# Routing a mixture of experts behind an attention: low parts of weights in halves, and the next round's maxima inside the tail of this one

## The chip, the cores and the metric

The kernel runs on one core of one Trainium2 chip. The metric is the device time of one execution in microseconds (us), as the median of several runs. Five engines work side by side, each through its own list of instructions, and wait for one another by semaphores: TensorE (PE in the profile; PEld is its loading of stationary operands), VectorE (DVE), ScalarE (ACT), GpSimd (POOL) and SyncE (SP, which here only starts transfers).

## The reference, cut to what matters

A local attention (4 batches, 8 heads, 768 positions, head size 64; window 16, and 24 block summaries) gives x of 3072 rows by 512. The rest is a mixture of 8 experts with a hard capacity:

```
def _moe_ref(x, w_gate, w1, w2):
    N, D = x.shape                     # 3072, 512
    E = w_gate.shape[1]                # 8
    cap = N // E                       # 384
    logits = x @ w_gate
    order = np.argsort(-logits.flatten())
    for idx in order:                  # greedy, from the largest logit down
        tok, e = (int(idx) // E, int(idx) % E)
        if assigned[tok] >= 0 or counts[e] >= cap:
            continue
        assigned[tok] = e
        counts[e] += 1
    for e in range(E):
        mask = assigned == e
        h = np.maximum(x[mask] @ w1[e], 0.0)     # 384 x 1024
        out[mask] = h @ w2[e]                    # 384 x 512
    return out
```

All experts get exactly 384 rows, and which rows they get depends on all the others.

## The kernel before

**Stages.** The attention takes about the first 145 us and writes x to memory and the logits to the tile `L` (128 x 24 tokens x 8 experts). After that come eight experts, one after the other. Expert r may only start when routing round r has said which expert fills up next (`widx`) and which rows it gets (`idx`). Round 0 runs alone, ahead of expert 0. Rounds 1 to 7 run under experts 0 to 5, cut into steps that are put between the matmuls of the experts.

**A round.** `aim` takes for each token the best logit among the experts still open (`best`), turns it into an integer key (`m`, `key`, `dup`), compares it with the first table of pivots (`g`), and finds which expert it belongs to (`cand`, `tgt`, one-hot `oh`). `search` then finds a threshold in six digits. A digit is 24 matmuls of the tables `g` with `oh` on TensorE (L449), `full` on VectorE (L451), one matmul with `steps` (L454), and on VectorE `piv`, two new tables `g` and `below` (L458 to L462). Between the third and the fourth digit stand `d`, `d`, `dup`, two `g` and `wh`. Behind the sixth come `wl`, `d`, `w`, `sel`, `widx`, two `ge` and two `inc` (L494 to L508), then two matmuls called px here (L522, L523), `place`, `to`, four `span`, the work of `spent` (which strikes out used-up experts in `WA`: `pos`, `keep`, `keep`, `WA`), twelve matmuls with `span` (L554, called at here), and `hit`, `m`, `hit`, `idx`. `close` (`wsum`, `pen`, `L`) takes the expert that is full out of `L`, and the next round's `aim` can begin.

**An expert.** Every fp32 operand is split into a high part (fp32r, made by ScalarE) and a low part (the difference, made by VectorE), and a product is three matmuls: high by high and the two mixed ones. The parts are `xh`, `xl` (gathered and transposed rows), `ah`, `al` (w1, four chunks), `hh`, `hl` (the hidden layer, 8 slices f), and `bh`, `bl` (w2, four chunks). The first half of an expert is 96 matmuls of 128 x 384, numbered h0 to h95 below, twelve for each slice f. The second half is 72 matmuls of 128 x 512, y0 to y71, nine for each f. The sums of the first half lie in three banks (`psum.tile(..., name="h", bufs=3)`, L744). So the matmuls of slice f + 3 can start only when `hh` and `hl` of slice f have been read out of the bank: h36 needs `hl` of f = 0, h48 that of f = 1, h60 that of f = 2, h72 that of f = 3. Rows for the next expert are transposed in four flips of three matmuls each (`flip_x`, L614) near the end of the second half, through one single bank `xt` (L615): a flip needs the `xl` of the flip before it, and that needs its `xh`.

**What sets the order.** Each engine works through its list strictly as the program writes it. The writing is done by a small planner in the kernel: `spend` adds the planned time of each matmul to `state["now"]`, `service` then writes out the delayed low parts in `later` whose due time has come (`hl` 1.1, `al` and `bl` 1.6, `xl` 1.1 after their high part was written), and calls `advance`, which writes the next step of the round once `state["ready"]` has passed. All of a step's VectorE instructions go into the list together. The numbers behind `yield` say after how long the next step's matmuls may be written. `prepare` starts the transfers of the next expert, its splits and its flips.

Of the kernel before, what the change touches and what calls it, by code (L numbers as in the profile page):

```python
# [33 lines left out]
NT = N // 128  # L34
VD = D + 1
TUNE = dict(
    hop=0.22, dv=1.0, e5=2, e50=0, warm2=3.6192, adv=14, y0=2.6, y1=0.3, y2=0.45,
    y2m=0.021, y3=1.7, y4=1.5, y5=1.6, y7=1.1, lo=1.1, sp=1.6, qx=23.421, aw=9.0, as_=2.6,
# [18 lines left out]
def attention_moe(ctx, tc, qT, kT, v65, wg, w1r, w2r, cst, out, dbg=None, dbi=None):  # L57
# [52 lines left out]

    def aim(T, t0, t1, last=False):
        n = t1 - t0
        best, cand, tgt = T["best"][:, t0:t1], T["cand"][:, t0:t1], T["tgt"][:, t0:t1]
        nc.vector.tensor_reduce(best, L[:, t0:t1], axis=AX.X, op=OP.max)
        ranks, experts = [], [
            lambda: nc.vector.tensor_tensor(cand, L[:, t0:t1], best[:, :, None].to_broadcast([128, n, E]), op=OP.is_equal),
            lambda: nc.vector.tensor_tensor(cand, cand, WA[:, t0:t1], op=OP.mult),
            lambda: nc.vector.tensor_reduce(tgt, cand, axis=AX.X, op=OP.max),
            lambda: nc.vector.tensor_scalar(tgt, tgt, 0.5, None, op0=OP.max)]
        if not last:  # L120
            m, key = T["m"][:, t0:t1], T["key"][:, t0:t1]
            bits = T["best"].bitcast(I32)[:, t0:t1]
            ranks = [
                lambda: nc.vector.tensor_scalar(m, bits, 31, 0x7FFFFFFF, op0=OP.arith_shift_right, op1=OP.bitwise_and),
                lambda: nc.vector.scalar_tensor_tensor(key, bits, 0x8000, m, op0=OP.bitwise_xor, op1=OP.bitwise_xor),
                lambda: nc.vector.tensor_copy(T["dup"][:, t0:t1], T["halves"][:, t0:t1, 1:2].to_broadcast([128, n, 2])),
                lambda: compare(T["g"], T["dup"], T["piv"], T["digits"][0], t0, t1)]
            experts.append(lambda: nc.vector.tensor_tensor(T["oh"][:, t0:t1], cand, tgt[:, :, None].to_broadcast([128, n, E]), op=OP.is_equal))
        for pair in zip_longest(ranks, experts):
            for op in pair:  # L130
                if op:
                    op()

# [331 lines left out]

    ROUND = {}

    def route(r):
        T = first
        if r:  # L470
            T = targets(r)
            aim(T, 0, NT, r == E - 1)
            yield 0.0, TUNE["y0"]
        R = psum.tile([128, 512], F32, name="r")
# [40 lines left out]

        late = TUNE["e5"] if r else TUNE["e50"]
        if r < E - 1 and not late:
            close()
        ROUND[r] = [widx, None]
        yield 0.03, TUNE["y4"]  # L520
        px = R[:, 32:34]
# [9 lines left out]
        def spent():  # L531
            if r == E - 1:
                return
            if late == 1:
                close()
            keep = rt.tile([128, NT], F32, name="keep", bufs=2)
            pos = rt.tile([128, NT], F32, name="pos", bufs=2)
            nc.vector.tensor_tensor(pos, place[:, 0, :NT], place[:, 1, :NT], op=OP.add)
            nc.vector.tensor_scalar(keep, pos, 0.5, None, op0=OP.is_lt)
            nc.vector.scalar_tensor_tensor(keep, pos, CAP + 0.5, keep, op0=OP.is_gt, op1=OP.add)  # L540
            nc.vector.tensor_tensor(WA, WA, keep[:, :, None].to_broadcast([128, NT, E]), op=OP.mult)
        m = ff.tile([128, 3, NT], F32, name="m3", bufs=2)
        hit = ff.tile([128, 3, NT + 1], F32, name="hit", bufs=2)
        idx = rt.tile([128, 3], I32, name="idx", bufs=E)
        for k in kinds:
            nc.vector.tensor_scalar(span[:, k, 0], count, px[:, k:k + 1], None, op0=OP.is_ge)
            nc.vector.tensor_scalar(span[:, k, 1], count, to[:, k:k + 1], -1.0, op0=OP.is_ge, op1=OP.mult)
        if r:
            spent()
        yield 0.05, TUNE["y5"]  # L550
        todo = [(k, i) for k in kinds for i in range(2)]
# [6 lines left out]
        with nc.allow_low_precision("integers below 2^24"):  # L558
            nc.vector.tensor_reduce(idx, hit, axis=AX.X, op=OP.add)
        if r == 0:  # L560
            spent()
        ROUND[r][1] = idx
        if r < E - 1 and late == 2:
            close()
# [19 lines left out]
    def split_w(r, nm, j, n=1, wait=TUNE["wlo"]):  # L584
        raw = RAW.pop((r, nm, j))
        hi = ff.tile([128, 1024], F32R, name=nm + "h", bufs=4)
        lo = ff.tile([128, 1024], F32R, name=nm + "l", bufs=4)
        WT[r, nm, j] = hi, lo
        for k in range(n):
            c = slice(k * 1024 // n, (k + 1) * 1024 // n)  # L590
            nc.scalar.activation(hi[:, c], raw[:, c], AF.Copy)  # L591

            def low(c=c):
                nc.vector.tensor_tensor(lo[:, c], raw[:, c], hi[:, c].bitcast(F32), op=OP.subtract)  # L594
# [18 lines left out]

    def flip_x(r, d):  # L614
        pt = psum.tile([128, 3, 128], F32, name="xt")  # L615
        for c in range(3):
            flip4(pt[:, c], XG[r, c][:, d * 128:(d + 1) * 128])
        split_x(r, d, pt)

    def split_x(r, d, pt):  # L620
        if d == 0:
            XT[r] = [ff.tile([128, 4, CAP], F32R, name=n) for n in ("xh", "xl")]
        xh, xl = XT[r]
        p = pt.rearrange("p c k -> p (c k)")
        nc.scalar.activation(xh[:, d], p, AF.Copy)  # L625

        def low():
            nc.vector.tensor_tensor(xl[:, d], p, xh[:, d].bitcast(F32), op=OP.subtract)
            vector(0.55)
        later.append((state["now"] + TUNE["xlo"], low))  # L630

# [3 lines left out]

    def flush():
        for it in later[:]:
            later.remove(it)
            it[1]()

    def service():
        while True:
            for it in [x for x in later if x[0] <= state["now"]]:
                later.remove(it)
                it[1]()
            if state["done"] < E - 1 and state["ready"] <= state["now"]:
# [91 lines left out]
    def expert(r):  # L738
# [3 lines left out]
        hl = ff.tile([128, 8, CAP], F32R, name="hl")  # L742
        for f in range(8):
            ph = psum.tile([128, CAP], F32, name="h", bufs=3)  # L744
            wh, wl = (w.rearrange("p (j d k) -> p j d k", j=2, d=4)[:, f % 2] for w in WT[r, "a", f // 2])
# [9 lines left out]
            def low(f=f, ph=ph):  # L755
                nc.vector.scalar_tensor_tensor(hl[:, f], ph, 0.0, hh[:, f].bitcast(F32), op0=OP.max, op1=OP.subtract)  # L756
                vector(0.55)
            later.append((state["now"] + TUNE["lo"], low))
            if f % 2 == 0:
                later.append((state["now"] + TUNE["sp"], lambda f=f: split_w(r, "b", f // 2)))  # L760
        py = [psum.tile([128, DM], F32, name="y", bufs=3) for c in range(3)]
# [84 lines left out]
```

## Time and profile before

| | us |
|---|---|
| median of 3 runs | 507.22 |
| the runs | 507.22, 510.45, 506.15 |
| the profiled execution | 508.25 |
| its span in the trace | 506.5 |
| TensorE busy in it | 463.3 |
| VectorE busy | 330.1 |
| ScalarE busy | 214.4 |
| granted TensorE clock, mean over the span | 0.95 |

The span runs from the first to the last instruction of the trace; the 1.75 us that the execution took beyond it lie around it. In a row of the timeline stand start, length (both in us), engine, line, operation, the tile written and the tiles read, and in brackets the engine's idle time ahead of it with what ended that wait. Rows of windows give for each engine the busy time in the stretch and the number of instructions, then the granted clock of TensorE.

### The profile page before, as it was taken

What the parts mean: (1) busy time and instruction counts of PE and PEld (TensorE: products, weight loads), DVE (VectorE), ACT (ScalarE), POOL (GpSimd) and SP (SyncE); (2) the same over time, 40 slices, a digit from 0 to 9 for tenths busy, and PEclk for the clock granted to TensorE, in tenths of its full rate; (3) what the DMA queues carried; (4) which work ended last, traced back from release to release, by engine and by line L of the source; (5) the groups of instructions that cost most, each with busy time, mean ns of one, the idle gap of its engine ahead of it and who ended that gap; (6) DMA issues with size and microseconds to landing.
All of it is one profiled execution on the core that took longest, in us unless ns stands there. A gap on an engine that the chain in (4) does not pass through costs nothing.

```text
span 506.5 us, 13149 instructions
## 1 busy us (share of the span) xinstructions
PE 463.3 (91%) x5160; PEld 388.6 (77%) x5160; DVE 330.1 (65%) x1293; ACT 214.4 (42%) x450; POOL 131.7 (26%) x199
## 2 busy tenths in 40 slices
PE   3799999999973899989989999899999999999993
PEld 2568687877853798779768878877987998988982
DVE  3278789977866786757865966777778462362510
ACT  1277667876810441243323513342351453453410
POOL 9547743614220300220202302300400500402011
PEclk8799999999985699979998999999999999999997
DMA  8999969211110821920641733723535445531001
GB/s 264 315 303 297 320 221 312 91 51 44 65 65 6 295 96 38 323 98 1 231 167 63 249 146 104 272 84 154 180 109 184 127 162 169 180 111 42 22 21 41
DMA packets 24157, 76.28 MB, mean 151 GB/s; under 512 B 3488, under 2 KB 3744, under 8 KB 23712
## 3 DMA queue, kind: packets, MB, share of 16 engines
q1 hardware_dynamic: 18336, 56.58, 33.9%
q0 software_dynamic: 5760, 18.88, 10.7%
q8 instruction: 40, 0.66, 0.6%
q14 instruction: 21, 0.17, 0.1%
HBM read 62.86 MB, written 12.58 MB: 149 GB/s over the span
## 4 chain that ended last, share of the span: by engine, by line
PE 73%; DVE 13%; issue 7%; POOL 4%; DMA 1%; ACT 0%; POOLq 0%; SPq 0%; ACTq 0%; DVEq 0%
PE h L749 21%; PE y L766 19%; PE o L348 5%; PE t L135 5%; PE s L312 5%; PE r L449 5%; PE x L135 2%; PE x L269 2%; PE l L354 2%; PE xt L135 2%; POOL vw L204 2%; DVE al L594 2%; DVE g L107 2%; POOL out L732 1%; PE x L279 1%
## 5 line engine op out<-in xcount | busy, mean ns | idle before, releaser
L766 PE MATMUL y<-bl,hh 128*128 128x512 f32 x192 | 78.6, 409 | 0.0
L766 PE MATMUL y<-bh,hl 128*128 128x512 f32 x192 | 77.4, 403 | 0.0
L766 PE MATMUL y<-bh,hh 128*128 128x512 f32 x192 | 76.6, 399 | 0.0
L732 POOL DMA_INDIRECT out<-y,idx x24 | 23.9, 996 | 197.6 <-ACT y L730 193.4
L753 ACT ACTIVATE hh<-h 128x384 fp32r<-128x384 f32 x64 | 31.5, 492 | 89.7 <-PE h L749 88.9
L749 PE MATMUL h<-xh,ah 128*128 128x384 f32 x256 | 60.5, 352 | 1.3 <-DVE hl L756 1.3
L327 ACT ACTIVATE pe<-sm,mx 128x118 f32<-128x118 f32 x192 | 57.7, 384 | 8.3 <-DVE mx L320 8.1
L749 PE MATMUL h<-xh,al 128*128 128x384 f32 x256 | 58.1, 346 | 0.0
L749 PE MATMUL h<-xl,ah 128*128 128x384 f32 x256 | 56.8, 340 | 0.0
L756 DVE SCALAR_TENSOR_TENSOR hl<-h,hh 128x384 fp32r<-128x384 f32 x64 | 35.3, 552 | 30.9 <-ACT hh L753 30.9
L320 DVE CUSTOM_DVE_ANT_0 sm<-s,cs 128x118 f32<-128x118 f32 x192 | 41.6, 275 | 17.1 <-PE s L312 16.3
L605 POOL DMA_INDIRECT xg<-xd,idx x24 | 25.5, 1064 | 96.5 <-issue 67.5
L625 ACT ACTIVATE xh<-xt 128x384 fp32r<-128x384 f32 x28 | 13.8, 491 | 82.4 <-PE xt L135 82.4
L749 PEld LDWEIGHTS h<-xh,ah 128*128 128x128 f32 x256 | 46.2, 194 | 2.8 <-DVE hl L756 1.7
L591 ACT ACTIVATE ah<-raw 128x1024 fp32r<-128x1024 f32 (+1 forms) x36 | 32.7, 957 | 32.0 <-DMA raw<-w1r 29.4
L749 PEld LDWEIGHTS h<-xh,al 128*128 128x128 f32 x256 | 46.1, 193 | 0.0
L749 PEld LDWEIGHTS h<-xl,ah 128*128 128x128 f32 x256 | 45.3, 189 | 0.0
L449 PEld LDWEIGHTS <-g 128*128 128x128 bf16 x1008 | 28.8, 97 | 18.0 <-DVE g L107 7.6
L766 PEld LDWEIGHTS y<-bh,hh 128*128 128x128 f32 x192 | 36.4, 190 | 6.8
L766 PEld LDWEIGHTS y<-bh,hl 128*128 128x128 f32 x192 | 36.4, 190 | 5.7
L766 PEld LDWEIGHTS y<-bl,hh 128*128 128x128 f32 x192 | 36.2, 188 | 5.8
L594 DVE TENSOR_TENSOR al<-raw,ah 128x1024 fp32r<-128x1024 f32 (+1 forms) x36 | 38.7, 1099 | 2.5 <-ACT ah L591 2.5
(129 smaller groups left out, 789.5 us busy)
## 6 DMA issues: line engine op xcount, KB each, us to landing
raw<-w1r SPq DMA_DIRECT2D x32, 512.0 KB, 4.5
raw<-w2r SPq DMA_DIRECT2D x32, 512.0 KB, 4.3
vw<-v SPq DMA_DIRECT2D x48, 195.0 KB, 7.7
kd<-kT SPq DMA_DIRECT2D x16, 399.0 KB, 5.8
xd<-x POOLq DMA_DIRECT2D x24, 256.0 KB, 3.6
qt<-qT SPq DMA_DIRECT2D x3, 1536.0 KB, 9.8
qt<-qT SPq DMA_DIRECT2D x3, 512.0 KB, 5.5
xg<-xd,idx POOLq DMA_INDIRECT x24, 3.7
```

Source lines behind the costliest of these rows:

```text
L135: nc.tensor.transpose(o, i, idn)
L320: nc.vector.tensor_tensor_reduce(sm[:, p], PS[u][:, p], m, -0.125, 3e38, op0=OP.add, op1=OP.min, accum_out=mx[:, p:p + 1])
L327: nc.scalar.activation(PE_[u][:, p], SM[u][0][:, p], AF.Exp, bias=SM[u][1][:, p:p + 1], scale=-1.0)
L449: nc.tensor.matmul(pc, g[t // HT][:, t % HT * n:t % HT * n + 128], oh[:, t], start=t == 0, stop=t == NT - 1)
L591: nc.scalar.activation(hi[:, c], raw[:, c], AF.Copy)
L594: nc.vector.tensor_tensor(lo[:, c], raw[:, c], hi[:, c].bitcast(F32), op=OP.subtract)
L605: nc.gpsimd.indirect_dma_start(out=x, out_offset=None, in_=xd, in_offset=bass.IndirectOffsetOnAxis(ap=idx[:, c:c + 1], axis=0))
L732: st = nc.gpsimd.indirect_dma_start(out=out, out_offset=bass.IndirectOffsetOnAxis(ap=ROUND[r][1][:, c:c + 1], axis=0), in_=y, in_offset=None)
L749: nc.tensor.matmul(ph, a[:, d], b[:, d], start=n == 0, stop=n == 11)
L753: nc.scalar.activation(hh[:, f], ph, AF.Relu)
L756: nc.vector.scalar_tensor_tensor(hl[:, f], ph, 0.0, hh[:, f].bitcast(F32), op0=OP.max, op1=OP.subtract)
L766: nc.tensor.matmul(py[c], a[:, f, s], b, start=f == 0 and i == 0, stop=f == 7 and i == 2)
```

## The change

Four things change.

1. A low part of a weight chunk that is delayed (`al` and `bl` of experts 1 to 7, `bl` of expert 0) is written as two instructions of 128 x 512 instead of one of 128 x 1024.
2. A delayed low part is not written as soon as it is due. `fits` asks whether by the planner's numbers VectorE can finish it within `gap` = 0.8 of the time at which the round's next step is ready; if not, it waits until its slack (1.2 for `hl`, 0.8 for `xl`, 4.0 for a weight's half) has run out. Ahead of a slice f the `hl` of slice f - 3 is written if it isn't yet, and ahead of a flip the `xl` that is left.
3. `aim` is cut into `aim_ranks` (up to the first tables `g`) and `aim_experts` (`cand`, `tgt`, `oh`). A new `turn` does `close` and `aim_ranks` of the next round. In rounds 1 to 6 it is written directly behind `inc`, ahead of `place`. `spent` is written ahead of the four `span`, and ends with `aim_experts` of the next round. In round 0 both stand behind `idx`.
4. The next round has no step of its own for `aim` any more (it had one that waited for `y0` = 2.6); its first digit may be written right after the last step of this round.

```
-    hop=0.22, dv=1.0, e5=2, e50=0, warm2=3.6192, ...
+    gap=0.8, ya=2.9, hop=0.22, dv=1.0, warm2=3.6192, ...
...
+        def turn():
             close()
+            AIMED[r + 1] = targets(r + 1)
+            aim_ranks(AIMED[r + 1], 0, NT, r + 1 == E - 1)
+
+        early = 0 < r < E - 1
+        if early:
+            turn()
         ROUND[r] = [widx, None]
-        yield 0.03, TUNE["y4"]
+        yield 0.03, TUNE["y4"], TUNE["ya"] if early else 0.0
...
             nc.vector.tensor_tensor(WA, WA, keep[:, :, None].to_broadcast([128, NT, E]), op=OP.mult)
+            aim_experts(AIMED[r + 1], 0, NT, r + 1 == E - 1)
+        if early:
+            spent()
...
-        if r:
-            spent()
-        yield 0.05, TUNE["y5"]
+        yield 0.05, TUNE["y5"] + (1.2 if early else 0.0)
...
-        yield 0.45, TUNE["y7"]
+        yield 0.45, 0.0, TUNE["y7"]
...
-                later.append((state["now"] + wait, low))
+                for h in range(2):
+                    piece = slice(h * 512, h * 512 + 512)
+
+                    def half(piece=piece):
+                        nc.vector.tensor_tensor(lo[:, piece], raw[:, piece], hi[:, piece].bitcast(F32), op=OP.subtract)
+                        vector(0.61)
+                    later.append((state["now"] + wait, half, 0.61, 4.0, "w"))
...
     def flip_x(r, d):
+        flush("x")
...
+    def fits(it):
+        now, (due, _, cost, slack, _) = state["now"], it
+        idle = state["gen"] is None or not cost
+        return idle or now >= due + slack or max(state["dve"], now + TUNE["hop"]) + cost <= state["ready"] + TUNE["gap"]
...
         for f in range(8):
+            flush(("h", f - 3))
             ph = psum.tile([128, CAP], F32, name="h", bufs=3)
```

**VectorE, expert 1, end of round 2.** In these names `h_4236` is the bank of slice 6 before, and `h_4169` that of slice 2 after the change. Before, behind the `inc` of the round stand one `hl` and at once `place`:

```order
L499 TENSOR_SCALAR widx_3882<-w_3881 1x1
L500 SCALAR_TENSOR_TENSOR ge_3883<-d_4066,sel_4274 128x24
L501 SCALAR_TENSOR_TENSOR ge_3883<-d_4066,sel_4274 128x24
L508 SCALAR_TENSOR_TENSOR inc_3884<-ge_3883 128x24 x2
L756 SCALAR_TENSOR_TENSOR hl_4059<-h_4236,hh_4058 128x384
L529 SCALAR_TENSOR_TENSOR place_2970<-inc_3884,r_3880,ge_3883 128x24 x2
```

After the change, `close` and `aim_ranks` of round 3 stand there:

```order
L512 TENSOR_TENSOR wsum_72<-wsum_72,w_3855 128x1
L514 TENSOR_SCALAR pen_4244<-cs_63,w_3855 128x8
L515 TENSOR_TENSOR L_67<-L_67,pen_4244 128x192
L114 TENSOR_REDUCE best_4247<-L_67 128x24
L118 TENSOR_SCALAR m_4251<-best_4247 128x24
L119 TENSOR_TENSOR cand_4248<-L_67,best_4247 128x192
L121 SCALAR_TENSOR_TENSOR key_4252<-best_4247,m_4251 128x24
L122 COPY dup_4253<-key_4252 128x48
L107 TENSOR_TENSOR g00_77<-dup_4253,piv0_74 128x384
L107 TENSOR_TENSOR g01_78<-dup_4253,piv0_74 128x384
L775 SCALAR_TENSOR_TENSOR hl_4103<-h_4169,hh_4102 128x384
L535 SCALAR_TENSOR_TENSOR place_2970<-inc_3858,r_3854,ge_3857 128x24 x2
```

Ten instructions moved ahead of the `hl` of slice 2, and the slice whose `hl` stands there is number 2 where it was number 6.

**VectorE, expert 2, end of round 3, after the change.** This is the end of the next such block: `h_4744` is the bank of slice 1, and all of `turn`, `place`, `spent` and `aim_experts` stand ahead of these rows.

```order
L130 TENSOR_SCALAR tgt_4801<-tgt_4801 128x24
L132 TENSOR_TENSOR oh_4802<-cand_4800,tgt_4801 128x192
L553 TENSOR_SCALAR span_4847<-count_2966,r_4410 128x384
L554 TENSOR_SCALAR span_4847<-count_2966,to_4846 128x384
L553 TENSOR_SCALAR span_4847<-count_2966,r_4410 128x384
L554 TENSOR_SCALAR span_4847<-count_2966,to_4846 128x384
L605 TENSOR_TENSOR bl_4779<-raw_4461,bh_4778 128x512
L775 SCALAR_TENSOR_TENSOR hl_4696<-h_4744,hh_4695 128x384
```

Behind the block come a half of `bl` and only then the `hl` of slice 1.

**TensorE, expert 1, after the change.** `h_4284` is the bank of slice 4, `h_4323` that of slice 5, and the wait on DVE in its first row is for the `hl` of slice 2 shown above.

```order
L768 MATMUL h_4284<-xh_3990,al_3961 128x384 x4
L528 LDWEIGHTS cb_64
L528 MATMUL r_3854<-inc_3858,cb_64 128x2 [waits DVE_49]
L529 LDWEIGHTS steps_65
L529 MATMUL r_3854<-inc_3858,steps_65 128x1
L768 MATMUL h_4284<-xl_3991,ah_3960 128x384 x4
L768 MATMUL h_4323<-xh_3990,ah_3960 128x384 [waits DVE_49]
```

So px now stands four matmuls of the expert ahead of h60; before it stood at h95, behind the last bank that is taken in this expert.

**VectorE, end of expert 0, the third digit of round 2.** Before, the four `xl` of the flips stood here with the undivided `al` between them:

```order
L594 TENSOR_TENSOR al<-raw,ah 128x1024
L628 TENSOR_TENSOR xl<-xt,xh 128x384
L594 TENSOR_TENSOR al<-raw,ah 128x1024
L451 TENSOR_SCALAR full<-r 128x8
L628 TENSOR_TENSOR xl<-xt,xh 128x384
L594 TENSOR_TENSOR al<-raw,ah 128x1024
L628 TENSOR_TENSOR xl<-xt,xh 128x384 x2
```

After:

```order
L455 TENSOR_SCALAR full<-r 128x8
L605 TENSOR_TENSOR al<-raw,ah 128x512
L484 TENSOR_SCALAR d<-key,below,r 128x24
L485 SCALAR_TENSOR_TENSOR d<-d,key 128x24
L487 TENSOR_SCALAR dup<-d 128x48
L107 TENSOR_TENSOR g_79<-dup,piv_74 128x384
L107 TENSOR_TENSOR g_80<-dup,piv_74 128x384
L491 SCALAR_TENSOR_TENSOR wh<-r,cs 128x8
L605 TENSOR_TENSOR al<-raw,ah 128x512
L639 TENSOR_TENSOR xl<-xt,xh 128x384 x2
L455 TENSOR_SCALAR full<-r 128x8
L605 TENSOR_TENSOR al<-raw,ah 128x512 x2
```

The first `xl` moved behind the routing work of the third digit, and the last two behind the `full` of the fourth. On TensorE the four flips stand at y60, y66, y69 and y72 now (y57, y66, y72, y72 before), with the third digit at y61, its `steps` matmul at y64, and the fourth digit at y71. In expert 3 the four flips stand at y30, y39, y51 and y63 (before: y27, y36, y45, y54), the sixth digit of round 5 at y35, its `steps` matmul at y39, and px at y51; between the `full` of that digit and the `xl` of the second flip stand a half of `al`, the first `xl`, another half, `wl` to `inc`, the whole `turn`, and two more halves.

The lists of GpSimd and SyncE hold the same instructions in the same order as before. TensorE's holds the same matmuls of the experts, the flips and the rounds, at other places.

More of the change, by code (lines that the diff above doesn't have):

```diff
@@ L109, in compare, with aim_ranks @@
                                         piv[:, None, :n].to_broadcast([128, b - a, n]).rearrange("p t (j k) -> p t j k", k=2), op=OP.is_ge)
-    def aim(T, t0, t1, last=False):
+    def aim_ranks(T, t0, t1, last=False):
         n = t1 - t0
-        best, cand, tgt = T["best"][:, t0:t1], T["cand"][:, t0:t1], T["tgt"][:, t0:t1]
+        best, cand = T["best"][:, t0:t1], T["cand"][:, t0:t1]
         nc.vector.tensor_reduce(best, L[:, t0:t1], axis=AX.X, op=OP.max)
[L115 to L119, printed above, removed]
         if not last:
@@ L122, in aim, with aim_experts @@
             bits = T["best"].bitcast(I32)[:, t0:t1]
[L123 to L132, printed above, removed]
+            nc.vector.tensor_scalar(m, bits, 31, 0x7FFFFFFF, op0=OP.arith_shift_right, op1=OP.bitwise_and)
+        nc.vector.tensor_tensor(cand, L[:, t0:t1], best[:, :, None].to_broadcast([128, n, E]), op=OP.is_equal)
+        if not last:
+            nc.vector.scalar_tensor_tensor(key, bits, 0x8000, m, op0=OP.bitwise_xor, op1=OP.bitwise_xor)
+            nc.vector.tensor_copy(T["dup"][:, t0:t1], T["halves"][:, t0:t1, 1:2].to_broadcast([128, n, 2]))
+            compare(T["g"], T["dup"], T["piv"], T["digits"][0], t0, t1)
+    def aim_experts(T, t0, t1, last=False):
+        n = t1 - t0
+        cand, tgt = T["cand"][:, t0:t1], T["tgt"][:, t0:t1]
+        nc.vector.tensor_tensor(cand, cand, WA[:, t0:t1], op=OP.mult)
+        nc.vector.tensor_reduce(tgt, cand, axis=AX.X, op=OP.max)
+        nc.vector.tensor_scalar(tgt, tgt, 0.5, None, op0=OP.max)
+        if not last:
+            nc.vector.tensor_tensor(T["oh"][:, t0:t1], cand, tgt[:, :, None].to_broadcast([128, n, E]), op=OP.is_equal)
+    def aim(T, t0, t1):
+        aim_ranks(T, t0, t1)
+        aim_experts(T, t0, t1)
     def flip4(o, i):
@@ L466, in attention_moe @@
     ROUND = {}
+    AIMED = {0: first}
     def route(r):
-        T = first
-        if r:
-            T = targets(r)
-            aim(T, 0, NT, r == E - 1)
-            yield 0.0, TUNE["y0"]
+        T = AIMED.pop(r)
         R = psum.tile([128, 512], F32, name="r")
@@ L533, in spent @@
                 return
-            if late == 1:
-                close()
             keep = rt.tile([128, NT], F32, name="keep", bufs=2)
@@ L560, in route @@
         if r == 0:
+            turn()
             spent()
         ROUND[r][1] = idx
-        if r < E - 1 and late == 2:
-            close()
         if dbi is not None:
@@ L629, in low @@
             vector(0.55)
-        later.append((state["now"] + TUNE["xlo"], low))
+        later.append((state["now"] + TUNE["xlo"], low, 0.55, 0.8, "x"))
     scat = []
@@ L634, in attention_moe, with flush @@
     later = []
-    def flush():
+    def flush(tag=None):
         for it in later[:]:
-            later.remove(it)
-            it[1]()
+            if tag is None or it[4] == tag:
+                later.remove(it)
+                it[1]()
+    def fits(it):
+        now, (due, _, cost, slack, _) = state["now"], it
+        idle = state["gen"] is None or not cost
+        return idle or now >= due + slack or max(state["dve"], now + TUNE["hop"]) + cost <= state["ready"] + TUNE["gap"]
     def service():
         while True:
-            for it in [x for x in later if x[0] <= state["now"]]:
-                later.remove(it)
-                it[1]()
+            for it in [x for x in later if x[0] <= state["now"] and fits(x)]:
+                if fits(it):
+                    later.remove(it)
+                    it[1]()
             if state["done"] < E - 1 and state["ready"] <= state["now"]:
@@ L757, in low @@
                 vector(0.55)
-            later.append((state["now"] + TUNE["lo"], low))
+            later.append((state["now"] + TUNE["lo"], low, 0.55, 1.2, ("h", f)))
             if f % 2 == 0:
-                later.append((state["now"] + TUNE["sp"], lambda f=f: split_w(r, "b", f // 2)))
+                later.append((state["now"] + TUNE["sp"], lambda f=f: split_w(r, "b", f // 2), 0.0, 0.0, "b"))
         py = [psum.tile([128, DM], F32, name="y", bufs=3) for c in range(3)]
```

5 lines of the change are left out of this document (1 added, 4 removed).

## The prediction, as it stood before the changed kernel ran

> **What bounds the kernel now.** I read the page first, then the windows over the stretch in which experts and routing rounds share the engines, then the waits of TensorE in it, and last the timeline at each wait.
>
> ```profile
> PE 463.3 (91%) x5160; PEld 388.6 (77%) x5160; DVE 330.1 (65%) x1293; ACT 214.4 (42%) x450; POOL 131.7 (26%) x199
> 172.00:396.00 224.00, 215.62 (x1894) 181.81 (x1895) 164.31 (x545) 80.09 (x123) 31.53 (x47) 0.97 0.43 150
> PE xt L135 <- DVE xl L628: 6.2, 6, 2.2
> PE h L749 <- DVE hl L756: 1.3, 1, 1.3
> 212.00:216.00 4.00, 2.71 (x14) 1.92 (x13) 3.66 (x7) 1.44 (x2) 0.00 (x0) 1.00 0.95 363
> 216.00:220.00 4.00, 3.24 (x34) 2.28 (x32) 2.54 (x6) 2.90 (x5) 2.36 (x3) 0.67 0.27 104
> 220.00:224.00 4.00, 3.59 (x13) 3.25 (x14) 2.14 (x7) 0.98 (x2) 1.11 (x3) 0.50 0.17 66
> 260.00:264.00 4.00, 1.88 (x11) 1.30 (x9) 1.92 (x9) 0.49 (x1) 0.00 (x0) 1.00 0.01 4
> 264.00:268.00 4.00, 3.92 (x36) 3.21 (x37) 0.64 (x2) 2.06 (x4) 1.89 (x3) 0.65 0.14 54
> 384.00:388.00 4.00, 2.94 (x25) 2.23 (x25) 3.90 (x11) 0.49 (x1) 0.00 (x0) 1.00 0.66 222
> ```
>
> TensorE is the bound. Under the rounds (172 to 396 us) it is idle for 224 - 215.62 = 8.4 us, and nearly all of that is waiting for VectorE: for `xl` at the flips, once for `hl`. VectorE is busy for 164 of the 224 us, so what matters is not its sum but what stands ahead of `xl` and `hl` in its list. The gaps lie at the end of expert 0 (1.29 + 0.76 + 0.41 = 2.46), of expert 1 (2.12, and 0.23 a little earlier), of expert 4 (1.06), and one of 1.34 in expert 3. A gap also costs clock: behind the first group TensorE was granted 0.67 and 0.50 for four microseconds each (some 3.3 us lost), behind the 2.12 it was granted 0.65 (1.4, and 0.3 in the next slice). The gaps of 1.34 and 1.06 cost no clock. So all that can be won is about 8.4 + 5.0 = 13.4 us.
>
> **How long the pieces last.** First the block that the change moves, from expert 3 (VectorE's timeline), with the wait of TensorE that ended on its last row; then the rows that give the distances between engines; last the paces.
>
> ```profile
> 310.76 0.23 DVE L494 SCALAR_TENSOR_TENSOR wl<-r,wh 128x8 f32<-128x8 f32 x1 [0.59 <-PE r L454]
> 311.94 0.31 DVE L508 TENSOR_TENSOR_SCAN inc<-ge 128x24 bf16<-128x24 f32 x2
> 312.67 0.41 DVE L529 SCALAR_TENSOR_TENSOR place<-inc,r,ge 128x24 f16<-128x24 bf16 x2 [0.42 <-PE r L523]
> 313.07 0.31 DVE L546 TENSOR_SCALAR span<-count,r 128x384 f16<-128x384 f16 x1
> 313.99 0.17 DVE L538 TENSOR_TENSOR pos<-place 128x24 f32<-128x24 f16 x1
> 314.91 0.55 DVE L756 SCALAR_TENSOR_TENSOR hl<-h,hh 128x384 fp32r<-128x384 f32 x1
> 315.37 0.15 DVE L555 COPY hit<-r 128x3 f32<-128x3 f32 x1
> 316.11 0.15 DVE L511 TENSOR_TENSOR wsum<-wsum,w 128x1 f32<-128x1 f32 x1
> 316.71 1.22 DVE L594 TENSOR_TENSOR bl<-raw,bh 128x1024 fp32r<-128x1024 f32 x1
> 317.85 0.34 DVE L114 TENSOR_REDUCE best<-L 128x24 f32<-128x192 f32 x1
> 319.80 0.26 DVE L119 TENSOR_SCALAR tgt<-tgt 128x24 bf16<-128x24 bf16 x1
> 320.36 1.01 DVE L756 SCALAR_TENSOR_TENSOR hl<-h,hh 128x384 fp32r<-128x384 f32 x2
> 320.97 0.96 PE L749 MATMUL h<-xh,ah 128*128 128x384 f32 x4 [1.34 <-DVE hl L756]
> 212.07 0.18 PE L454 MATMUL r<-full,steps 128*128 128x9 bf16 x1
> 212.30 0.32 DVE L458 TENSOR_SCALAR piv<-cs,r,below 128x64 int16<-128x64 f32 x1 [1.21 <-PE r L454]
> 213.66 1.22 DVE L594 TENSOR_TENSOR al<-raw,ah 128x1024 fp32r<-128x1024 f32 x1
> 214.79 0.55 DVE L628 TENSOR_TENSOR xl<-xt,xh 128x384 fp32r<-128x384 f32 x1
> 215.49 0.52 PE L135 MATMUL xt<-cs,xg 128*128 128x128 f32 x3 [1.29 <-DVE xl L628]
> 216.05 0.49 ACT L625 ACTIVATE xh<-xt 128x384 fp32r<-128x384 f32 x1 [2.58 <-PE xt L135]
> 216.08 0.76 PE L449 MATMUL r<-oh,g 128*128 128x8 bf16 x24
> 216.88 0.17 DVE L451 TENSOR_SCALAR_CACHE_REDUCE full<-r 128x8 bf16<-128x8 f32 x1 [0.40 <-PE r L449]
> 222.67 0.30 DVE L483 TENSOR_SCALAR d<-key,below,r 128x24 f32<-128x24 int16 x1 [0.24 <-PE r L454]
> 223.59 0.63 DVE L107 TENSOR_TENSOR g<-dup,piv 128x384 bf16<-128x384 int16 x2
> 167.44 2.50 DVE L594 TENSOR_TENSOR al<-raw,ah 128x512 fp32r<-128x512 f32 x4 [1.26 <-ACT ah L591]
> 190.82 0.60 PE r L449 x24
> 430.30 16.66 PE h L749 x96
> 446.96 6.17 PE y L766 x27
> ```
>
> From these: an h matmul 16.66 / 96 = 0.174 us, a y matmul 6.17 / 27 = 0.229, a digit 0.60 (0.7 with the slower first matmul behind it). `full` starts 0.80 after its digit, VectorE answers `steps` after 0.23, `hl` lets TensorE go 0.61 after its start, `xl` 0.70. `wl` to the end of `inc` 1.4. `close` 0.60, and 0.1 more where `best` must wait for `L`. All of `aim` 320.36 - 317.85 = 2.5, of which the part now in `aim_ranks` is taken as 1.55 (between 1.4 and 1.95). `turn` is then 2.25. `place` to `span` 0.40, four `span` 0.92, `pos` to `WA` 0.92. From `wsum` to the last `span` of the new order: 0.7 + 2.5 + 0.40 + 0.92 + 0.92 = 5.45. A half weight 2.50 / 4 = 0.62, an `hl` 0.46.
>
> **The change part by part.**
>
> *Halves.* 60 instructions of 1.22 become 120 of 0.62: some 1.2 us more of VectorE work in all, none of it by itself on the path. I cost it at nothing; VectorE's idle time (60 us in the stretch) covers it, except where a half stands ahead of `xl` or `hl`, which is counted there.
>
> *The block ahead of `hl`.* I count from the start of the sixth digit. In expert 1 (digit at h39, `steps` after 5 matmuls: 0.7 + 0.87 = 1.57, px at h56) `wl` starts at 1.8, `turn` ends at 1.8 + 1.4 + 2.25 = 5.45, and the `hl` of slice 2 frees TensorE at 6.05. TensorE is at h60 at 0.7 + 21 x 0.174 + 0.2 = 4.55: a gap of 1.5. The `hl` of slice 3 stands behind the rest of the block (3.2) and a half: it frees TensorE at 10.4, while h72 is due at 6.05 + 2.08 = 8.1: a gap of 2.3. In expert 2 (digit at h17, `steps` at h20, px at h32) the block ends at 1.45 + 1.4 + 5.45 = 8.3, a half and `hl` later TensorE may go at 9.5; h48 is due at 6.3: a gap of 3.2. In expert 3 (digit at y71 of expert 2, px at h12) `hl` of slice 0 frees TensorE at 1.5 + 1.4 + 5.45 + 0.61 = 9.0, h36 is due at 7.4: a gap of 1.6 in place of the 1.34 of before. Together 3.8 + 3.2 + 0.3 = 7.3 us. The 1.34 of before is itself such a case: there `wsum` to `oh` and a `bl` stood ahead of the `hl` at 320.36. I trust these gaps to some 20%.
>
> *The flips.* End of expert 0, from the third digit at y61: `full` at 0.8, a half until 1.5, `d` at 1.6 (after `steps` at y64), first `g` 0.92 later, the two `g` and `wh` until 3.2, a half until 3.85, `xl` frees the second flip at 4.55. It is due at 1.9: 2.65. The third flip follows the second by 0.56 + 0.49 + 0.70 = 1.8 and is due after 0.95: 0.85. The fourth waits for the fourth digit, its `full` and two halves: 3.6 against 1.6: 2.0. With 0.2 at the first h matmuls 5.7, before 2.46. End of expert 3, from the digit at y35: the first `xl` stands behind `full` and a half and frees the second flip at 2.2 (due 1.65); the second stands behind a half, `wl` to `inc`, `turn` and two halves: 2.0 + 0.62 + 1.4 + 2.25 + 1.24 = 7.5, so the third flip goes at 8.2 (due 5.3); the third `xl` stands behind `place` to `span`: 11.9 (due 11.2). Together 4.1; before nothing that counts. In the same way, from the third digit: in expert 2 three halves, `d`, `g` and `wh` stand ahead of the first `xl`, which frees the second flip at 5.3 (due 4.0): 1.3 (before 0.1). In expert 1, where the halves do stand better, only the fourth flip is late, behind the third digit's `d`, `g` and `wh`: 1.1 (before 2.35). In expert 4 two halves stand ahead of each `xl`: 1.4 (before 1.06). The flips: 13.6 against 6.0, so +7.6 us.
>
> *The start.* Round 0's `oh` no longer waits behind four pieces of `al`, and `idx` comes some 0.4 earlier because `close` left its path. I take 0.7 us won, between 0 and 1.5.
>
> *Round ends.* Rounds gain nothing: where the first digit of the next round is written earlier, its last one stands within a few matmuls of where it stood, and TensorE's work is the same. Rounds 1 to 7 cover experts 0 to 5 in both. The transfers stand in the same order on SyncE and GpSimd; `idx` comes later by the block, which the 5 us and more between the gathers and the first flip cover.
>
> *The clock.* Before, it lost 5.0 us. After, four gaps or groups are above the 2.12 that cost 1.7 (expert 0's end, expert 1, expert 2, expert 3's end). At 1.7 to 3.3 each that is 6.8 to 13, less the 5.0 and less what VectorE's chains hide while TensorE is slow. I take +3, between -1 and +8.
>
> *The sum.* 7.3 + 7.6 - 0.7 + 3 = 17.2 us. The profiled execution took 508.25, so 525.4; it lies 1.0 above the median of the runs shown (507.22), so a median of 507.2 + 17 = 524.
>
> **The rivals.** *The clock holds.* All new gaps except that of 3.2 are clearly shorter, and two gaps above 1 us cost no clock before. If no new gap costs any: 507.2 + 14.2 - 5.0 = 516. Against it stands the row of 0.65 behind the 2.12, so 15%. The Trainium skill has this rule ("TensorE: Matmul & The Clock Gate", Part 1): the clock falls to half after an idle window of about 3.4 us. By it hardly any gap here would cost clock, and the trace disagrees at 2.12. *The flips are as before.* If the halves between them cost no more than the undivided `al` did, only the block ahead of `hl` remains: 507.2 + 7.3 - 0.7 = 514. 10%. *Faster.* If what stands ahead of `xl` at the ends of experts 0 and 1 goes and nothing else happens, 2.46 + 2.35 + 5.0 + 0.7 = 10.5 us are won: 497. For it: in both places an undivided `al` stands directly ahead of the late `xl`. It needs `turn` to take under 0.75 us instead of 2.25, for then h60 isn't late. 5%. *Nothing comes of it.* Gaps and gains cancel, 507. 5%. *The clock stays low.* Each of five places loses 3.3: 14.2 + 16.5 - 5.0 = 25.7, so 533. 10%.
>
> **How the numbers follow.** The forecast has 55%. I take 524, and 513 to 532 as the range: that leaves out the two cases at the fast end and half of the slowest. About 1% (5 us) is what a measurement of this kernel can tell from no change. Faster by more than that 5%; within it 8% (the case of nothing, and the near end of the one of 514); slower 87%.
>
> **What would show it.** Each step has a wait of its own: in the profile after, TensorE waits for `hl` some five times for about 8.5 us in all (before once, 1.3), the longest in expert 2 at its fifth slice; for `xl` about 13 us (before 6.2), the longest at the third flip of expert 3 and the second of expert 0. TensorE is idle for 20 to 25 us under the rounds, and the granted clock is low behind at least three of these places. I am wrong if h60 of expert 1 starts without a gap, or if the flips at the end of expert 0 follow one another without one.

## The result, and the profile after

| | before | after |
|---|---|---|
| median of 4 runs, us | 507.81 | 523.91 |
| the runs | 507.22, 510.45, 506.15, 508.39 | 524.64, 524.87, 523.16, 523.01 |
| the profiled execution, its span | 508.25, 506.5 | 524.64, 522.6 |
| first matmul of round 0 | 146.93 | 149.78 |
| h0 of expert 0 | 174.07 | 176.99 |
| y0 of expert 5 | 412.33 | 428.46 |

The changed kernel takes 1.031 times as long (95% interval 1.026 to 1.036). The last three rows are starts in the timeline. They split the 16.1 us of span: 2.85 lie ahead of round 0, where the two programs differ only in the order inside `aim`, 0.07 between there and expert 0, and 13.2 from there to the middle of expert 5 (251.47 against 238.26). From y0 of expert 5 on nothing differs. Of the runs behind the ratios further below two were in a slower state and are left out: one of 879 us among the second experiment's four, and one of 515 us of the kernel before beside the ninth and tenth.

The page of the kernel after, busy time of each engine:

```profile
PE 466.6 (89%) x5160; PEld 391.2 (75%) x5160; DVE 338.3 (65%) x1353; ACT 214.5 (41%) x450; POOL 130.8 (25%) x199
```

Its windows: the stretch of the rounds, which now ends at 416, and the slices behind the gaps.

```profile
172.00:416.00 244.00, 223.71 (x1929) 188.75 (x1930) 173.50 (x596) 81.91 (x126) 35.10 (x53) 0.96 0.41 143
220.00:224.00 4.00, 3.53 (x36) 2.30 (x36) 0.87 (x4) 1.96 (x4) 1.65 (x3) 0.75 0.27 105
224.00:228.00 4.00, 2.60 (x10) 2.01 (x10) 2.19 (x5) 0.98 (x2) 0.66 (x3) 0.50 0.17 66
228.00:232.00 4.00, 4.00 (x27) 3.84 (x27) 1.41 (x5) 1.44 (x2) 0.80 (x1) 0.89 0.17 66
244.00:248.00 4.00, 1.98 (x6) 1.98 (x7) 3.50 (x9) 0.26 (x1) 0.00 (x0) 0.74 0.41 164
248.00:252.00 4.00, 4.00 (x30) 3.84 (x30) 0.53 (x3) 1.44 (x2) 0.00 (x0) 0.83 0.00 0
284.00:288.00 4.00, 0.78 (x5) 0.46 (x3) 3.79 (x14) 0.64 (x2) 0.00 (x0) 0.86 0.99 398
288.00:292.00 4.00, 3.88 (x12) 3.88 (x13) 1.60 (x4) 0.00 (x0) 0.00 (x0) 0.50 0.07 30
292.00:296.00 4.00, 4.00 (x30) 3.69 (x29) 1.70 (x6) 1.87 (x3) 0.16 (x1) 0.79 0.00 0
360.00:364.00 4.00, 1.48 (x11) 1.00 (x9) 3.86 (x15) 0.00 (x0) 0.00 (x0) 1.00 0.76 251
```

TensorE stands idle for 244 - 223.71 = 20.3 us of the stretch (before 8.4). Its busy time counts slow matmuls too, so the lost clock has to be read apart: busy time by 1 - granted clock, summed over the slices, is 2.6 + 1.2 + 2.9 = 6.7 us behind expert 0's end, in expert 1 and in expert 2. The same sum for before is 4.6 (the rows in the prediction, and 0.97 and 0.93 in the slices from 224 and 268). At the start of expert 0 each kernel lost about 1.5 more. The waits in that stretch (engine, line, releaser: us in all, times, longest):

```profile
DVE hit L560 <- PE r L559: 15.9, 5, 4.6
...
PE xt L139 <- DVE xl L639: 9.6, 9, 2.5
PE h L768 <- DVE hl L775: 8.7, 4, 3.3
```

TensorE's timeline at the waits for `hl` (h60 and h72 of expert 1, h48 of expert 2, h36 of expert 3) and at the largest ones for `xl`:

```profile
241.38 0.96 PE L768 MATMUL h<-xh,ah 128*128 128x384 f32 x4 [1.30 <-DVE hl L775]
246.02 1.33 PE L768 MATMUL h<-xh,ah 128*128 128x384 f32 x3 [2.28 <-DVE hl L775]
288.12 1.33 PE L768 MATMUL h<-xh,ah 128*128 128x384 f32 x3 [3.34 <-DVE hl L775]
332.06 0.97 PE L768 MATMUL h<-xh,ah 128*128 128x384 f32 x4 [1.80 <-DVE hl L775]
...
219.91 0.52 PE L139 MATMUL xt<-cs,xg 128*128 128x128 f32 x3 [2.24 <-DVE xl L639]
225.68 0.87 PE L139 MATMUL xt<-cs,xg 128*128 128x128 f32 x3 [1.40 <-DVE xl L639]
363.68 0.55 PE L139 MATMUL xt<-cs,xg 128*128 128x128 f32 x3 [2.52 <-DVE xl L639]
```

And VectorE ahead of the row at 288.12, where the block ends and a half of `bl` still comes first:

```profile
285.71 0.36 DVE L132 TENSOR_TENSOR oh<-cand,tgt 128x192 bf16<-128x192 bf16 x1
...
286.69 0.31 DVE L554 TENSOR_SCALAR span<-count,to 128x384 f16<-128x384 f16 x1
286.91 0.68 DVE L605 TENSOR_TENSOR bl<-raw,bh 128x512 fp32r<-128x512 f32 x1
287.52 0.55 DVE L775 SCALAR_TENSOR_TENSOR hl<-h,hh 128x384 fp32r<-128x384 f32 x1
```

### The profile page after: what moved, and what is told of

Same layout as the page of the kernel before. It is cut to its first block, busy times and chain, and to the rows that moved or that the text cites. A ratio compares the mean times of both kernels' runs of the same rounds, so it can differ in the third digit from the quotient of the medians.

```text
span 522.6 us, 13202 instructions
## 1 busy us (share of the span) xinstructions
PE 466.6 (89%) x5160; PEld 391.2 (75%) x5160; DVE 338.3 (65%) x1353; ACT 214.5 (41%) x450; POOL 130.8 (25%) x199
## 4 chain that ended last, share of the span: by engine, by line
PE 70%; DVE 17%; issue 7%; POOL 4%; POOLq 0%; ACT 0%; DVEq 0%; ACTq 0%
PE h L768 22%; PE y L785 18%; PE t L139 5%; PE r L453 5%; PE o L352 5%; PE s L316 5%; PE x L139 2%; PE l L358 2%; PE x L273 2%; POOL vw L208 2%; PE xt L139 2%; DVE g L107 2%; DVE al L605 2%; PE x L205 1%; POOL out L750 1%
## 5 line engine op out<-in xcount | busy, mean ns | idle before, releaser
L768 PE MATMUL h<-xh,al 128*128 128x384 f32 x256 | 60.3, 352 | 0.0
L768 PE MATMUL h<-xl,ah 128*128 128x384 f32 x256 | 58.7, 348 | 0.0
L768 PEld LDWEIGHTS h<-xh,ah 128*128 128x128 f32 x256 | 47.3, 198 | 10.6 <-DVE hl L775 10.0
L768 PEld LDWEIGHTS h<-xh,al 128*128 128x128 f32 x256 | 47.6, 198 | 0.0
L768 PEld LDWEIGHTS h<-xl,ah 128*128 128x128 f32 x256 | 46.4, 195 | 0.0
L605 DVE TENSOR_TENSOR bl<-raw,bh 128x512 fp32r<-128x512 f32 x64 | 42.0, 684 | 0.0
```

The source lines that it names most:

```text
L605: nc.vector.tensor_tensor(lo[:, piece], raw[:, piece], hi[:, piece].bitcast(F32), op=OP.subtract)
L768: nc.tensor.matmul(ph, a[:, d], b[:, d], start=n == 0, stop=n == 11)
```

## The experiments

Each kernel ran beside the kernel before, in one set on one chip. In three of the four sets (all experiments but the ninth and tenth) the kernel before took 517 to 518 us, in the other 508.8. The three ran on the chip that the record numbers 0, the other on chip 12; for the first pair no number is on record. The expectations in us were worked out from a kernel before of 507. Waits are those of TensorE between 172 and 420 us.

The slower sets have something that the first pair and the set of 508.8 have not: VectorE stops. From the fifth experiment, which is the kernel before itself, GpSimd's, VectorE's and TensorE's timeline early in expert 4:

```profile
366.70 0.94 POOL L605 DMA_INDIRECT xg<-xd,idx  x1 [0.31 <-issue]
...
368.92 0.17 DVE L451 TENSOR_SCALAR_CACHE_REDUCE full<-r 128x8 bf16<-128x8 f32 x1 [5.96 <-remote]
...
369.15 0.17 PE L454 MATMUL r<-full,steps 128*128 128x9 bf16 x1 [4.76 <-DVE full L451]
```

Its digit had ended at 363.8. In the ten profiles of those sets I count 41 such waits of VectorE (nearly all at `full`) that the profile puts down to no work of the round, but to "remote" or to matmuls of an expert; in the other four profiles (before, after, ninth, tenth) there is none. So a ratio from the slower sets also holds the stops that a kernel met there. They need not be chance: the eighth and eleventh experiments, which are one kernel, met the same two (2.51 and 5.00 us, 2.50 and 5.00). The column of stops gives their number and their sum on VectorE. What a kernel's own order does is read from its waits for `hl` and `xl`.

| experiment | ratio, 95% interval | waits for `hl` | for `xl` | stops |
|---|---|---|---|---|
| 1 halves alone | 0.994, 0.991 to 0.997 | 0.6 | 6.3 | 5, 13.5 |
| 2 deferral, old round | 1.014, 1.005 to 1.022 | 0 | 12.6 | 3, 9.4 |
| 3 new round, old low parts | 1.019, 1.010 to 1.028 | 8.8 | 8.2 | 7, 17.5 |
| 4 new round, `hl`, `xl` first | 0.991, 0.987 to 0.995 | 4.3 | 4.8 | 3, 6.0 |
| 5 the kernel before again | 0.999, 0.995 to 1.002 | 1.8 | 6.4 | 5, 13.3 |
| 6 the changed kernel again | 1.024, 1.016 to 1.031 | 8.9 | 9.2 | 5, 11.5 |
| 7 as 4, block cut | 0.991, 0.987 to 0.994 | 0 | 7.3 | 5, 13.0 |
| 8 old round, `hl`, `xl` first, `aim` cut | 0.984, 0.978 to 0.990 | 0 | 3.2 | 2, 7.5 |
| 9 changed kernel, gaps filled | 1.023, 1.018 to 1.028 | 0.9 | 8.4 | 0 |
| 10 as 8, `aim` whole | 0.993, 0.989 to 0.996 | 0 | 3.3 | 0 |
| 11 as 8 again | 0.984, 0.978 to 0.991 | 0 | 3.2 | 2, 7.5 |
| 12 as 10 again | 1.004, 1.000 to 1.008 | 0 | 3.4 | 4, 14.2 |

**Which part costs: 1, 2 and 3.** The first adds only the halves to the kernel before:

```
-                later.append((state["now"] + wait, low))
+                for h in range(2):
+                    ...
+                    later.append((state["now"] + wait, half))
```

> The kernel before with one edit alone: each delayed low part of a weight chunk is written as two instructions of 128 x 512, both as soon as they are due. The round and its order are as before. Theory (the block of turn and spent ahead of hl costs most, the deferral the rest): two halves take 2 x 0.62 = 1.24 us on VectorE against 1.22 for one, so the list is the same in time; TensorE waits for xl 6 us and for hl 1 to 2 us as before, and the time is that of before within 2 us. Rival (halves cost by themselves, by their fixed part or by blocking): over 511 us. Second rival (the halves alone already win at the flips): under 505.

It came out 3 us below the kernel before. That is a little more than the 2 us that the theory allowed, and by the time alone it is the second rival's case; but the waits for `xl` are those of the kernel before, so nothing was won at the flips, and there were as many stops. Where the 3 us come from was not found. So the halves are not what costs. The second keeps halves, `fits` and flushes, and puts the round back:

```
-        early = 0 < r < E - 1
-        if early:
-            turn()
...
+        T = targets(r)
+        aim_ranks(T, 0, NT, r == E - 1)
+        aim_experts(T, 0, NT, r == E - 1)
+        yield 0.0, TUNE["y0"]
```

> The changed kernel with the round put back as it was (spent behind the four span, close behind idx, the whole aim in a step of its own with its wait of 2.6), while the halves, the deferral by fits and the flushes ahead of a slice and of a flip stay. Theory: the 8.7 us of waiting for hl go to under 2, because no block stands ahead of hl; the flips keep part of their loss, some 6 to 9 us waited for xl; time 507 to 512. Rival (the deferral is what costs, the place of the block does not matter): 518 to 524, with waits for hl still at 5 us or more.

The waits for `hl` are gone, as the theory has it, but those for `xl` rose to 12.6 us where it had 6 to 9, and the time (some 7 us above the kernel before) lies between theory and rival. VectorE's timeline of this kernel at the end of expert 3:

```profile
348.70 3.70 DVE L602 TENSOR_TENSOR al<-raw,ah 128x512 fp32r<-128x512 f32 x6
...
354.91 0.36 DVE L132 TENSOR_TENSOR oh<-cand,tgt 128x192 bf16<-128x192 bf16 x1
355.19 0.69 DVE L602 TENSOR_TENSOR al<-raw,ah 128x512 fp32r<-128x512 f32 x1
355.79 0.55 DVE L636 TENSOR_TENSOR xl<-xt,xh 128x384 fp32r<-128x384 f32 x1
```

and the flip that waited for its last row:

```profile
356.39 0.90 PE L139 MATMUL xt<-cs,xg 128*128 128x128 f32 x3 [4.28 <-DVE xl L636]
```

Six halves that had been put off came out in a row, then all of `aim`, then one more half, and only then the `xl`. So a half that waits for a gap does not vanish: it comes later, together with others, at a place that nobody chose. The third has the new round with the old rule for low parts:

```
-        return idle or now >= due + slack or ...
+        return True
...
-            flush(("h", f - 3))
-        flush("x")
```

with chunks undivided again.

> The changed kernel with the low parts as they were before (undivided chunks, each low part written as soon as it is due, no flush ahead of a slice or a flip), while the round keeps turn ahead of place and spent with aim_experts ahead of span. Theory: the block still stands ahead of hl, so TensorE still waits for hl some 6 to 9 us; with undivided pieces among them the flips cost about what they cost before, 6 to 8 us; time 514 to 522. Rival (the deferral is what costs): 506 to 511, with waits for hl under 2 us.

It met the theory, but for 8.2 us of waits for `xl` where that had 6 to 8: the block alone brings the waits for `hl`, undivided chunks or not. So both parts of the change make waits by themselves, the deferral at the flips and the block at the banks. In the changed kernel they don't add up: 9.2 us for `xl` against 12.6 with the deferral alone.

**Drift: 5 and 6**, the two kernels unchanged.

> The kernel before, unchanged, beside itself: what two runs of one program differ by, and the stages on the chip of these experiments. Theory (the 2.4 us by which the attention of the changed kernel's profiled execution came later are drift between executions and nothing of the change): the first matmul of round 0 lies anywhere between 145 and 150 us, ratio 1.00 within 0.005. Rival (the attention of the kernel before is always earlier): 145.5 to 147.0.

> The changed kernel, unchanged, beside the kernel before on this chip. Theory (the loss is in the order of VectorE's list, so it goes with the program): ratio 1.022 to 1.037, waits for hl 7 to 10 us, for xl 8 to 11. Rival (part of the loss was of that chip or that profiled execution): ratio 1.00 to 1.015 with the same waits.

The first matmul of round 0 came at 148.10 here for the kernel before and at 147.46 for the changed one, so the order of the two is turned round: the 2.85 us of the first pair are for the most part drift of executions, not the change. A small part does belong to it. VectorE's piece of `aim` that stands ahead of a copy to `L` takes 1.92 us in the profile after and 1.48 in that of before, since its two parts no longer alternate, and TensorE's last logits wait for that copy: 1.09 us against 0.65 in the first pair, 1.09 against 0.66 in this one. The changed kernel's loss was there again (0.0235, within the theory), with the same waits to some tenths.

**What goes first: 4, 7 and 8.** The fourth keeps the changed round and alters the rule. A weight's half goes only where VectorE is free, `hl` and `xl` go at once, ahead of any half:

```
-        return idle or now >= due + slack or max(state["dve"], ...) + cost <= state["ready"] + TUNE["gap"]
+        return tag != "w" or now >= due + slack or state["dve"] <= now + TUNE["hop"]
...
-            for it in [x for x in later if x[0] <= state["now"] and fits(x)]:
+            for it in sorted([...], key=lambda x: x[4] == "w"):
...
         if early:
+            flush("h")
             turn()
```

> The changed kernel with its round, and with another rule for what goes first on VectorE: hl and xl are written as soon as they are due and ahead of any weight piece; a weight's half is written only when VectorE is free by the planner's numbers or its slack of 4.0 has run out; and every hl that is waiting is written ahead of turn, ahead of place and behind spent. Theory: in expert 1 the hl of slice 2 now stands ahead of turn and that of slice 3 ahead of place, in expert 2 that of slice 1 ahead of place; waits for hl fall from 8.7 to under 3 us, waits for xl to 4 to 7, the clock losses behind them to under 5 us in all; time 507 to 513. Rival (the block is too long for three banks in whatever order hl stands): hl waits stay above 6 us and the time above 518.

The waits for `hl` halved, between theory and rival; the time is below the kernel before, though with 6.0 us of stops against its 13.3 that is not all of its own making. The seventh also cuts the block, by writing the `span` behind `to` and `spent` as a step of its own:

```
+            yield 0.05, 1.7
+            spent()
+            yield 0.0, 2.4
```

> The kernel of the fourth experiment (changed round, hl and xl first, a weight's half only where VectorE is free) with its block cut: the four span stand directly behind place and to, then spent with aim_experts as a step of its own, so that the planner can write an hl between turn, span and spent. Theory (the length of what stands unbroken ahead of hl makes the wait, three banks give 6.2 us for an hl): the 4.3 us of waits for hl left there go to under 1.5, for xl 3 to 6; ratio 0.975 to 0.990 against the kernel before. Rival (the round's end itself is later and pushes the next flips): hl waits go, but xl waits rise to over 8 and the ratio is 0.99 to 1.01.

The waits for `hl` went to nothing: it was the unbroken length that made them. Those for `xl` rose from 4.8 to 7.3, and the ratio did not move. Theory and rival are each half right. The eighth leaves the early `turn` out (shown against the round of the second experiment):

```
             aim_ranks(T, 0, NT, r == E - 1)
+            yield 0.0, 1.7
             aim_experts(T, 0, NT, r == E - 1)
-            yield 0.0, TUNE["y0"]
+            yield 0.0, 1.2
```

> The round in the old order (place, span, spent, then hit to idx with close, then aim), but aim cut into aim_ranks and aim_experts as two steps, with hl and xl first and a weight's half only where VectorE is free. Theory (what matters is what stands ahead of hl and xl, not where turn stands): waits for hl under 1, for xl 3 to 6 us; ratio 0.975 to 0.990. Rival (the early turn is what wins once low parts go first): 0.99 to 1.005, slower than the kernel of the seventh experiment by over 1%.

It has the fewest waits for `hl` and `xl` of all and is 1.6% below the kernel before. The early `turn` is not needed for it.

**The cut through `aim`: 10, 11 and 12.** The tenth is the eighth without that cut.

> The kernel of the eighth experiment with aim in one piece again (one step of 3 us on VectorE with its wait of 2.6): the old round as it was before, hl and xl first, a weight's half only where VectorE is free. It tells how much of that kernel's 1.6% is the order of the low parts and how much the cut through aim. Theory (the order of the low parts is what wins, since hl stood ahead of aim there already): waits for hl under 1, for xl 3 to 7 us, ratio 0.980 to 0.992. Rival (the cut in aim is what wins): 0.995 to 1.01, with hl or xl behind oh in VectorE's list and over 8 us of such waits.

> The kernel of the eighth experiment once more, beside that of the tenth on one chip, since the two were timed on different chips (0.984 and 0.993). Theory (the cut through aim wins some 3 us on its own, because no xl and no first digit stands behind an undivided aim of 3 us): 0.980 to 0.989 here. Rival (the two are the same and the chips differ): both within 0.004 of each other.

> The kernel of the tenth experiment once more, beside that of the eighth on one chip. Theory (the cut wins on its own): 0.990 to 0.996, with one wait for xl of about 3 us behind oh near the end of expert 3 as before. Rival (the chips differ): 0.980 to 0.989, like its neighbour.

The tenth came out at 0.993, just outside the theory (to 0.992), with its waits as the theory had them. The eleventh repeated the eighth; the twelfth missed both its expectations. From h0 of expert 0 to y0 of expert 5 it took 249.2 us, where the same kernel had taken 232.6 in the tenth, with the same waits for `xl`. In between lie the stops: one of 3.82 and one of 5.35 us among them, with a granted clock of 0.50 behind both. The eighth and eleventh met two stops each and took 237.1 and 238.3. On that chip the kernel with the cut is 12 us faster, with 6.7 us fewer of stops; that the cut wins by itself, where there are no stops, is not shown. What it surely saves is some 1.2 us at the start, where the first digit waited 2.1 to 2.3 us for `oh` and with the cut 0.6 to 0.7. Free of stops, the halves and the order of the low parts are together worth 0.7% (the tenth): 232.6 us in the stretch against 238.3 before and 251.5 after. Halves alone came out at 0.994 in the first experiment, in another set, so the ratios don't say how much of this is the order. Its waits speak for the order: 3.3 us for `hl` and `xl` together, against 6.9 with halves alone and 7.5 before.

**The clock: 9.** Matmuls that nobody reads fill the changed kernel's four gaps for `hl`:

```
+            fill = {(1, 5): 20, (1, 6): 36, (2, 4): 54, (3, 3): 28}.get((r, f), 0)
+                    nc.tensor.matmul(spare[:, 0], upper_b, upper_b, start=True, stop=True)
```

> The changed kernel, and in its four gaps ahead of h60 and h72 of expert 1, h48 of expert 2 and h36 of expert 3 TensorE gets 20, 36, 54 and 28 matmuls of 128 x 128 whose result nobody reads (into the bank of the flips, which is free there). They need nothing but TensorE; 45 like them took 4.41 us at the start at a clock of 0.50 to 0.79, so at full clock I estimate 0.05 to 0.06 us each and gaps filled to nine tenths. Theory (it is TensorE's standing idle that costs the clock behind these gaps): the clock stays at 0.97 or more in the slices behind the gaps of experts 1 and 2 (in the changed kernel 0.74 and 0.83, then 0.86, 0.50 and 0.79, about 4 us lost), the waits for hl are gone from the list, and the time is 2 to 5 us below that of the changed kernel, ratio 1.015 to 1.028 against the kernel before. Rival (the clock falls for another reason): 0.50 to 0.85 in the same slices, ratio 1.025 to 1.04. Second rival (the fillers run longer than the gaps): the matmul behind them waits for nothing and starts over 0.5 us later than it did.

Its windows at the two places where the changed kernel had 0.74, 0.83 and 0.86, 0.50, 0.79:

```profile
244.00:248.00 4.00, 3.83 (x42) 3.60 (x41) 3.76 (x17) 0.91 (x2) 0.00 (x0) 1.00 0.98 386
248.00:252.00 4.00, 3.74 (x30) 3.57 (x28) 2.36 (x5) 0.70 (x2) 0.00 (x0) 1.00 0.16 64
284.00:288.00 4.00, 4.00 (x49) 3.84 (x48) 3.72 (x17) 1.93 (x3) 0.00 (x0) 1.00 0.81 328
288.00:292.00 4.00, 3.70 (x36) 3.53 (x34) 2.98 (x7) 0.08 (x1) 0.00 (x0) 1.00 0.47 189
292.00:296.00 4.00, 4.00 (x55) 3.69 (x54) 2.83 (x8) 1.85 (x3) 1.14 (x1) 1.00 0.01 2
```

The clock held in these slices: it is the idling that costs it. The first half of expert 2 fell from 25.88 to 23.35 us, which is nearly the 2.9 that the windows had put down to the clock there. In expert 1 the part from h72 on fell from 6.21 to 4.72, but the half as a whole did not (25.93 against 26.02), since it began at a clock of 0.50. The end of expert 0, with gaps of 2.24 and 1.40 as in the profile after, had lost more clock in this execution: 0.50 in three slices, where that had it in one. So in the profiled execution h0 of expert 0 to y0 of expert 5 took 250.9 us, only 0.5 less than the 251.5 of the profile after. The median, 521.1 beside 508.8, is 2.8 below that of the changed kernel in the first pair, the ratio within what the theory gave; but the changed kernel without fillers was not in this set, so what the fillers save in time is less sure than what they do to the clock.

## Why the prediction was right

The number (524 against 523.9) fits better than its terms do. The signs were as foretold in kind: four waits for `hl` with 8.7 us in all (some five and 8.5 foretold), 9.6 us for `xl` (about 13), 20.3 us of idle time (20 to 25).

| step | predicted | measured |
|---|---|---|
| block ahead of `hl`: gaps of 1.5, 2.3, 3.2, 1.6 | +7.3 | 1.30, 2.28, 3.34, 1.80: +7.4 |
| flips: 13.6 against 6.0 | +7.6 | 9.6 against 6.2: +3.4 |
| the start | -0.7 | +0.1 |
| the clock | +3 | 6.7 against 4.6: +2.1 |
| ahead of round 0 | 0 | +2.85 |
| sum | 17.2 | 15.9 of 16.1 |

*The block ahead of `hl`* was right in every place to 0.2 us (the sum of gaps is less the 1.34 of before), and the third experiment shows that it is the new round that makes these gaps, the second that they go with it.

*The flips* were the term that was mis-sized. The places were right, the late `xl` in expert 0 (2.65, 0.85, 2.0 predicted; 2.24, 0.47, 1.40 measured) and in expert 3 (0.55, 2.9, 0.7; 0.38, 2.52, 0.72), but nearly every gap was taken 0.2 to 0.6 too long (also those of 1.1 and 1.3 in experts 1 and 2, which came out as 0.74 and 0.87), and in expert 4 1.4 came out as 0.29. Each count began at a digit and took TensorE's matmuls up to the flip at their bare pace, which makes the flip due too early. Counted from the same digits in the profile after, four of these flips (the second of expert 0, the second and third of expert 3, the second of expert 2) came due at 2.14, 1.80, 5.52 and 4.31, where the forecast had 1.9, 1.65, 5.3 and 4.0, and went at 4.38, 2.18, 8.04 and 5.17, where it had 4.55, 2.2, 8.2 and 5.3. So the due time was 0.15 to 0.31 too early, and that is the larger part of the error; VectorE's part was 0.02 to 0.17 too long. What failed in expert 4 was not counted in this way.

*The start* was wrong: `oh` no longer stands behind the four pieces of `al`, but the `full` of the first digit does now, and TensorE waits 1.24 us for it with the last flip and h0 behind:

```profile
175.47 0.17 PE L458 MATMUL r<-full,steps 128*128 128x9 bf16 x1 [1.24 <-DVE full L455]
```

Counted from the first matmul of round 0, the first digit of round 1 came 2.3 us earlier than before, but h0 0.07 us later: the gain was given back at once. Some 0.4 us were lost in round 0 itself, where the first `steps` matmul came 2.33 instead of 1.92 behind that first matmul, because it now waits for `oh`.

*The clock* came out within its bounds, and the rival in which it holds is refuted by the 0.50 at 288. (The 2.12 that the prediction reads off before is the idle time of a slice; the gap itself was 2.21.) That idling is the cause is shown by the ninth experiment; what a given gap costs was luck (below).

*The 2.85 us ahead of round 0* were not foreseen, and all but some 0.4 of them are no part of the change. They made up for most of what the flips were too large by, which was luck. Without them the changed kernel stands at about 521, well in the range; the change itself costs some 13 us, which is also about what its second measurement says (0.0235 of 517 is 12).

That nothing is gained by the early `turn` was right: the kernels with the fewest waits (eighth and tenth) are without it.

## What to carry to other kernels

Where one engine's list serves both a chain that another engine waits for and bulk work, put the pieces that free a buffer (here `hl` and `xl`) ahead of everything, and write bulk only where the engine is free. Before moving a block earlier, count what stands unbroken ahead of the next such piece against the time that the buffers give. Work that is put off for a better gap needs a place where it does land; otherwise it lands in a heap ahead of something that is waited for.

## What was not expected of the hardware

**The same gap costs clock in one execution and none in the next.** At the end of expert 3 the changed kernel's flip waited 2.52, 2.54 and 2.51 us in its three profiles (after, sixth, ninth). The row of 360 above and the one behind it have a clock of 1.00; the sixth has 0.63 in the slice from 364, the ninth 0.89 and 0.69. The Trainium skill ("TensorE: Matmul & The Clock Gate", Part 1) says that activity is watched over a free-running window, so that the same kernel may show it differently from run to run; these rows agree. Its figure for a window without work, about 3.4 us, is longer than gaps that cost clock here (2.28 in expert 1, with 1.30 ahead of it).

**VectorE stops while GpSimd starts indirect DMAs, in some sets only.** Each of the 41 stops lies over one to four indirect DMAs of GpSimd and ends between 0.95 us before and 1.5 us behind the end of one. All stand ahead of instructions that wait for a matmul of the round (37 `full`, two `place`, one `piv`, one `hit`), so it can be the release of the wait that is late. In the four profiles without stops 30 `full` started within such a DMA or up to 0.5 us behind one, and none was late; in the ten with stops 23 more lay so without a stop. So the overlap alone isn't enough, and no run changed these DMAs. Stops were seen on chip 0 alone; whether it is the chip or something else of these sets stays open. What such a set costs, stops and the clock behind them, shows where one kernel is in both: 16.6 us of stretch in the tenth and twelfth, 12.5 in the first profile of before (238.3) and the fifth (250.8; that execution, of 521.9 us, was its slowest, and by medians it is 9).

**VectorE now waits too.** `hit` waited 16.4 us in all for the matmuls of at (2.1 before), up to 4.6 at once, since at is written later and `hit` holds up the list. No wait of TensorE could be traced to it.
